# Two interleaved side pipelines of a fused attention and channel-mix kernel, moved from a 12-step to a 14-step beat

## Chip, cores and metric

The kernel runs on one core of one Trainium2 chip. The metric is device time in microseconds (us); less is better. The kernel's main loop has 400 steps of some 2.8 us each.

## What is computed

```python
def mab(q, kv):                          # m = 32 inducing points, C = 128, N = 12608, B = 4
    s = scale * (q @ kv.transpose(0, 2, 1))
    s = s - s.max(-1, keepdims=True)
    a = np.exp(s); a /= a.sum(-1, keepdims=True) + 1e-09
    return a @ kv
h = mab(I, x)                            # 32 pooled rows per batch, needs all of x
x = mab(x, h)                            # every token attends to the 32 rows
x_prev = shift x by one token
xk = mu_k * x + (1 - mu_k) * x_prev;  xr = mu_r * x + (1 - mu_r) * x_prev
k = np.maximum(xk @ w_k, 0)              # 128 -> 1024
out = sigmoid(xr @ w_r) * (k * k @ w_v)  # 1024 -> 128
```

## The kernel before

**The main loop.** The tokens of a batch are cut into 24 groups of 512 and one of 320, and a group's 1024 hidden columns into four units of 256. A step handles one unit of one group, so a batch has 25 x 4 = 100 steps (`UB`) and the program 400, counted n = 0 to 399. In a step TensorE first does the up projection of unit n (four matmuls into `ps_a`, L773 and L775), VectorE takes the positive part into `k_t` (L785), ScalarE squares it twice (`kh`, L790, and the exact square over `k_t`, L791), GpSimd takes the difference `kl` of the two (L793), and TensorE does the down projection of unit n - 4 (six matmuls into `ps_v`, L804). In the steps listed in `high_vector`, VectorE makes `kh` (L787) in place of ScalarE. In steps with n mod 4 = 1 TensorE also computes the gate's input (`zgate`, L762 and L763) into the `ps_v` bank that the group's down projection will use next, and ScalarE reads it for the sigmoid `rT` (L765); the first down matmul of that group, in step n + 3, overwrites the bank and so has to wait for `rT`. VectorE multiplies the finished group by `rT` (`gate`, L809, n mod 4 = 0) and transposes it into the output tile `ot` (L820, n mod 4 = 1). `ot` has one buffer for four groups, stored by four DMAs (L827) in steps 16k + 5; the next four groups begin to fill it in step 16k + 9 and wait for those DMAs.

Every engine executes its instructions in the order in which the Python code issues them. `ps_a` has two buffers, so the up projection of step n + 2 waits for VectorE's reads of step n.

**The side pipelines.** Two chains of small operations are hung into the steps by hand: `at(n, f)` runs f at the end of step n, `soon(n, f)` runs it right after the up projection of step n.

- `stage_a(b, j, at, t)` folds block j (2048 tokens) of batch b into the running softmax of the 32 pooled rows. It transposes the block on VectorE in four pieces (`btr`, L333, into `xs`) and moves each piece by four DMAs into the tiles `xt` (L336); at t + 9 come scores on TensorE (L361, bank `pb_a`) and a maximum on VectorE (L364); `common` (L371, bank `pb_b`) and `running` at t + 11; `expo` on ScalarE at t + 15; a transpose `e1` at t + 17 (L405); `hmm`, 16 small matmuls each, at t + 18 and t + 19 (L426); `acc` at t + 20. The last full block takes the 320 left-over tokens along (`t_scores`, and L370 before `common`), one step later.
- `stage_b(b, j, at, t)` computes the attention of block j's tokens over the finished rows: scores at t (L610, bank `pb_b`, kept until `low`), a softmax over 32 on VectorE with `expo` on ScalarE at t + 3 (L627), a high part `ah` at t + 7 (L650), a low part `al` at t + 9 (L654), and from t + 10 on, four times, `spread(i)`: five DMAs that build the tile `R` of one group (one for its first column out of the group before, L587, and four, L664). The main loop reads `R` in that group's four steps.
- `combine(b)` turns the pooled rows into the batch's weights `W` (t + 9 to t + 15).

All these DMAs and the loads of x go through SyncE's one queue (SP), in order. While the main loop works on batch b, stage A runs on batch b + 1 and stage B on the next blocks of batch b. ScalarE's `Exp` and `Sigmoid` need different tables, so a change from one to the other brings an `ACT_TABLE_LOAD`.

**The beat before** is one block per 12 steps (`SEG = 12`). With t = 100b (t = 4 for batch 0), stage A of block j starts at t + 12j and stage B of block j + 1 at t + 12j + 1; `combine` starts at t + 72 and stage B of the next batch's first block at t + 85.

Of the kernel before, what the change touches and what calls it, by code (L numbers as in the profile page):

```python
# [8 lines left out]
F32 = mybir.dt.float32  # L9
# [10 lines left out]
def kernel(  # L20
# [31 lines left out]
    xt_pool = ctx.enter_context(tc.tile_pool(name="xt_pool", bufs=24))  # L52
    st = ctx.enter_context(tc.tile_pool(name="st", bufs=1))
    wp = ctx.enter_context(tc.tile_pool(name="wp", bufs=2))
    sm = ctx.enter_context(tc.tile_pool(name="sm", bufs=2))
    r_pool = ctx.enter_context(tc.tile_pool(name="r_pool", bufs=10))
    mp = ctx.enter_context(tc.tile_pool(name="mp", bufs=2))
    pa = ctx.enter_context(tc.tile_pool(name="pa", bufs=2, space=bass.MemoryType.PSUM))
    pv = ctx.enter_context(tc.tile_pool(name="pv", bufs=2, space=bass.MemoryType.PSUM))
# [19 lines left out]
    wr_sb = const.tile([P, C], F32, name="wr_sb")  # L79
# [223 lines left out]
    def xt_tile(S, j, i):  # L303

        w = groups(j)[0][1]
        if w == G:
            S.xt[j, i] = xt_pool.tile([P, G], F32, name="xt")
        elif i == 0:
            S.xt_tail = xt_pool.tile([P, TAIL], F32, name="xtl", bufs=1)
            for ii in range(Q):  # L310
                S.xt[j, ii] = S.xt_tail[:, ii * w:(ii + 1) * w]
        return S.xt[j, i]

    def stage_a(b, j, at, t):
# [6 lines left out]
        S = batches[b]  # L321
# [4 lines left out]
        last = 4 if tail else 0  # L326

        def btr(c):
            if c == 0:
                for i in range(Q):  # L330
                    xt_tile(S, j, i)
            xs = st.tile([P, G], F32, name="xs", bufs=3)
            nc.vector.transpose(out=xs.rearrange("p (s q) -> p s q", q=M),  # L333
                                in_=S.xb[j][:, :, M * c:M * (c + 1)])
            for i in range(Q):
                nc.sync.dma_start(out=S.xt[j, i][M * c:M * (c + 1), :], in_=xs[M * i:M * (i + 1)])  # L336

        def t_tr():
            ps = pb_tile("a")
# [65 lines left out]
            nc.vector.transpose(out=L["e1"], in_=L["e1t"].rearrange("p (s q) -> p s q", q=M))  # L405

        def t_etrans():
            ps = pb_tile("b")
            nc.tensor.transpose(out=ps[:tw, :P], in_=L["s1t"], identity=ident)
            L["e1x"] = sm.tile([P, P], F32, name="mk", bufs=1)  # L410
            nc.vector.tensor_copy(out=L["e1x"][:tw], in_=ps[:tw, :P])
# [59 lines left out]
    def combine(b, at=None, t=0):  # L471
# [18 lines left out]
        def weights():  # L490
            ws = S.sum
            if ahead:
                wt = sm.tile([P, 1], F32, name="wt")
                nc.scalar.activation(out=wt, in_=S.mrun, func=AF.Exp, bias=L["nm"], scale=scale)
                ws = sm.tile([P, 1], F32, name="ws")
                nc.vector.tensor_tensor(out=ws, in0=S.sum, in1=wt, op=ALU.mult)
            ps = pb_tile(None if ahead else "b")
            nc.tensor.matmul(out=ps[:, :1], lhsT=stack_f, rhs=ws, start=True, stop=True)
            rd = sm.tile([P, 1], F32, name="rd")
            nc.vector.tensor_scalar(out=rd, in0=ps[:, :1], scalar1=EPS, scalar2=None, op0=ALU.add)  # L500
            nc.vector.reciprocal(out=rd, in_=rd)
            sw = sm.tile([P, P], F32, name="mk", bufs=1)
            if ahead:
                nc.vector.tensor_scalar(out=sw, in0=stack_f, scalar1=wt, scalar2=rd,
                                        op0=ALU.mult, op1=ALU.mult)
            else:
                nc.vector.tensor_scalar(out=sw, in0=stack_f, scalar1=rd, scalar2=None, op0=ALU.mult)
            L["sw"] = sw

        def hfin():  # L510
            ps = pb_tile(None if ahead else "b")
            nc.tensor.matmul(out=ps[:, :P], lhsT=S.acc, rhs=L["sw"], start=True, stop=True)
            h = sm.tile([P, P], F32, name="hT")
# [58 lines left out]

        if ahead:
            return maxes, weights, hfin, wpart
        at(t + 9, weights)
        at(t + 10, hfin)
        parts = [(s, f"k{s}", c * G, wk_sb[:, c * G:(c + 1) * G]) for c in range(F // G) for s in range(2)]
        for n in range(0, len(parts), Q):
            wpack(parts[n:n + Q], G, ("ah", "al", 1), t + 11 + 4 * (n // Q))
        wpack([(s, f"r{s}", F, wr_sb) for s in range(2)], C, ("xs", "xs", 3), t + 13)  # L580

    def halo(S, g, far=True):

# [5 lines left out]
            nc.vector.tensor_copy(out=S.R[g][:, 0:1], in_=S.R[g - 1].bitcast(F32)[:, G:G + 1])  # L589


    def stage_b(b, j, at, t):

# [60 lines left out]
        def spread(i):  # L656
            src = (L["ah"].bitcast(F32), L["al"].bitcast(F32))
            if full or i == 0:
                S.R[j * Q + i] = r_pool.tile([P, G + 1], F32R, name="R")
                halo(S, j * Q + i)  # L660
            R = S.R[j * Q + (i if full else 0)].bitcast(F32)
            o, lo = (0, 0) if full else (offs[i], i * w - offs[i])
            for q in range(Q):
                nc.sync.dma_start(out=R[M * q:M * (q + 1), 1 + o + lo:1 + o + w],  # L664
                                  in_=src[q % 2][M * i:M * (i + 1), lo:w])

        at(t, scores)
        at(t + 1, trans)
        at(t + 1, maxi)
        at(t + 2, sub)  # L670
        at(t + 3, expo)
        at(t + 5, total)
        at(t + 5, recip)
        at(t + 6, mult)
        at(t + 6, back)
        at(t + 7, high)
        at(t + 9, low)
        for i in range(Q):
            at(t + 10 + i, lambda i=i: spread(i))
# [256 lines left out]
    def at(n, f):  # L936
        events.setdefault(n, []).append(f)
# [39 lines left out]
            at(k + 5, put)  # L977
        at(4, lambda: units[0][0].zgate(first=True))

    SEG = 12  # L980
    high_vector = set()
    for b in range(B):
        t = b * UB + (4 if b == 0 else 0)
        for j in range(NBLK - 1):
            s = t + SEG * j
            high_vector |= {s + 4, s + 8}
            if b + 1 < B:
                stage_a(b + 1, j, at, s)
# [78 lines left out]
```

## Time and profile before

| | |
|---|---|
| time, median of 3 runs | 1167.95 us (1167.78 to 1170.74) |
| time of the profiled execution | 1165.47 us |
| its span, first to last instruction | 1163.7 us |
| instructions in the span | 17576 |
| main loop's first step begins at | 54.98 us |
| PE, PEld, DVE, ACT, POOL busy | 96%, 72%, 80%, 83%, 81% |
| mean granted TensorE clock | 0.996 |
| VectorE `kh` steps (L787) | 48 |
| table loads of ScalarE in the sigmoid, stage A and stage B lines (L765, L393 and L394, L627) | 31, 15 and 3, 12 |

PE is TensorE's matmuls and PEld its weight loads, DVE is VectorE, ACT ScalarE, POOL GpSimd, SPq the DMA issues of SyncE's queue. A row of the waits names the waiting engine with its tile and line, then what ended the wait, the total in us, the count and the longest. In the timeline a row has its start, its length and, in brackets, the idle time before it and what ended that. Ends of matmuls are modelled and overlap, so the distance from one start to the next tells more than their lengths.

### The profile page before, as it was taken

To read this page: it belongs to the slowest core of one execution; us is meant where nothing else is said; L and a number is where in the kernel's file an instruction comes from. 1 tells how busy PE (TensorE), PEld (TensorE's weight loads), DVE (VectorE), ACT (ScalarE), POOL (GpSimd) and SP (SyncE) were. 2 spreads that over 40 slices of the span, in tenths; PEclk is the share of its full clock that TensorE was granted. 3 is DMA by queue.
4 is the path that set the end of the run, shared out by engine and by line. 5 is a ranking of instruction groups with operands and counts; after the bars stand their busy time and mean duration, and the time that the engine had idled before them with its cause. 6 is when DMAs were issued, how large, how long until landed. Compare 5 with 4: busy or idle time off the path is not lost.

```text
span 1163.7 us, 17576 instructions
## 1 busy us (share of the span) xinstructions
PE 1114.2 (96%) x5746; PEld 834.2 (72%) x5746; DVE 934.3 (80%) x1259; ACT 970.9 (83%) x1107; POOL 947.7 (81%) x413
## 2 busy tenths in 40 slices
PE   7779999999999999999999999999999999999997
PEld 5456777776677777777767777777768777777886
DVE  5778889887878888888787889897787888887665
ACT  5478888887888888788978988888789888889996
POOL 1158888888787888888879888888878899999997
PEclk9989999999999999999999999999999999999999
DMA  9112554544226455465043554645304314432231
GB/s 288 50 32 75 128 118 106 109 117 92 39 58 134 108 105 123 108 135 120 5 76 74 118 125 104 134 96 124 45 15 82 63 34 73 73 64 46 43 46 34
DMA packets 273515, 102.31 MB, mean 88 GB/s; under 512 B 232816, under 2 KB 248336, under 8 KB 271120
## 3 DMA queue, kind: packets, MB, share of 16 engines
q1 hardware_dynamic: 273088, 101.17, 40.5%
q8 instruction: 46, 0.75, 0.3%
q14 instruction: 45, 0.37, 0.1%
q10 hardware_dynamic: 336, 0.02, 0.0%
HBM read 28.07 MB, written 25.82 MB: 46 GB/s over the span
## 4 chain that ended last, share of the span: by engine, by line
PE 61%; DVE 15%; ACT 8%; SPq 6%; issue 5%; DMA 4%; DVEq 0%; ACTq 0%
PE ps_v L804 31%; PE ps_a L773 11%; PE ps_a L775 10%; DVE k_t L785 5%; SPq L336 2%; DMA out_dram<-ot 2%; ACT kh L790 2%; SPq L827 2%; PE pb_a L426 1%; PE pb_b L610 1%; PE ps_v L762 1%; PE ps_v L763 1%; SPq L664 1%; ACT k_t L791 1%; PE pb_a L361 1%
## 5 line engine op out<-in xcount | busy, mean ns | idle before, releaser
L793 POOL TENSOR_TENSOR kl<-k_t,kh 128x1024 fp32r<-128x1024 f32 (+2 forms) x400 | 939.0, 2375 | 169.0 <-ACT k_t L791 148.9
L785 DVE TENSOR_SCALAR k_t<-ps_a 128x1024 f32<-128x1024 f32 (+1 forms) x400 | 480.9, 1202 | 155.5 <-PE ps_a L775 144.1
L791 ACT ACTIVATE k_t<-k_t 128x1024 f32<-128x1024 f32 (+1 forms) x400 | 418.2, 1048 | 45.5 <-DVE kh L787 34.3
L790 ACT ACTIVATE kh<-k_t 128x1024 fp32r<-128x1024 f32 (+1 forms) x352 | 365.9, 1040 | 104.5 <-DVE k_t L785 57.8
L773 PE MATMUL ps_a<-R,W 128*128 128x512 f32 (+1 forms) x800 | 325.9, 408 | 4.7 <-DMA R<-al 3.4
L775 PE MATMUL ps_a<-R,W 128*128 128x512 f32 (+1 forms) x800 | 313.6, 392 | 0.0
L804 PE MATMUL ps_v<-kh,wvh 128*128 128x512 f32 (+1 forms) x800 | 251.9, 396 | 5.5 <-ACT rT L765 5.0
L804 PE MATMUL ps_v<-kl,wvh 128*128 128x512 f32 (+1 forms) x800 | 249.2, 393 | 0.0
L804 PE MATMUL ps_v<-kh,wvl 128*128 128x512 f32 (+1 forms) x800 | 249.0, 392 | 0.0
L773 PEld LDWEIGHTS ps_a<-R,W 128*128 128x128 f32 x800 | 151.2, 189 | 82.3 <-issue 22.4
L804 PEld LDWEIGHTS ps_v<-kh,wvh 128*128 128x128 f32 x800 | 147.9, 189 | 42.3 <-ACT rT L765 10.1
L804 PEld LDWEIGHTS ps_v<-kl,wvh 128*128 128x128 f32 x800 | 149.6, 188 | 35.5 <-POOL kl L793 0.3
L804 PEld LDWEIGHTS ps_v<-kh,wvl 128*128 128x128 f32 x800 | 149.8, 188 | 34.9
L775 PEld LDWEIGHTS ps_a<-R,W 128*128 128x128 f32 x800 | 151.1, 189 | 29.8
L820 DVE STREAM_TRANSPOSE ot<-oT 128x512 f32<-128x512 f32 x96 | 67.4, 702 | 12.2 <-DMA out_dram<-ot 11.3
L809 DVE TENSOR_TENSOR oT<-ps_v,rT 128x512 f32<-128x512 f32 (+1 forms) x100 | 66.7, 667 | 2.4 <-PE ps_v L804 0.2
L787 DVE SCALAR_TENSOR_TENSOR kh<-ps_a,k_t 128x1024 fp32r<-128x1024 f32 x48 | 58.8, 1225 | 5.4 <-PE ps_v L804 0.5
L765 ACT ACTIVATE rT<-ps_v 128x512 f32<-128x512 f32 (+1 forms) x99 | 57.2, 578 | 0.3
L333 DVE STREAM_TRANSPOSE xs<-xb 128x512 f32<-128x512 f32 x72 | 50.0, 695 | 0.3
L765 ACT ACT_TABLE_LOAD x31 | 39.8, 1283 | 0.6
L762 PE MATMUL ps_v<-R,W 128*128 128x512 f32 (+1 forms) x99 | 38.9, 393 | 0.0
L763 PE MATMUL ps_v<-R,W 128*128 128x512 f32 (+1 forms) x99 | 38.7, 391 | 0.0
(194 smaller groups left out, 643.6 us busy)
## 6 DMA issues: line engine op xcount, KB each, us to landing
out_dram<-ot SPq DMA_DIRECT2D x92, 256.0 KB, 4.4
xb<-in_x_dram SPq DMA_DIRECT2D x18, 1024.0 KB, 5.3
xt<-xs SPq DMA_DIRECT2D x288, 64.0 KB, 2.0
R<-ah SPq DMA_DIRECT2D x184, 64.0 KB, 2.0
R<-al SPq DMA_DIRECT2D x184, 64.0 KB, 2.0
kh<-in_x_dram SPq DMA_DIRECT2D x4, 512.0 KB, 8.2
kl<-in_x_dram SPq DMA_DIRECT2D x4, 512.0 KB, 6.4
xb<-in_x_dram SPq DMA_DIRECT2D x8, 256.0 KB, 5.4
```

The lines of the kernel that those rows point to most:

```text
L762: nc.tensor.matmul(out=ps[:, :w], lhsT=S.W[0][:, F:WF], rhs=R[:, 1:w + 1], start=True, stop=False)
L765: nc.scalar.activation(out=self.rT, in_=ps[:, :w], func=AF.Sigmoid)
L773: nc.tensor.matmul(out=ps[:, c, :w], lhsT=S.W[0][:, cs], rhs=R[:, 1:w + 1], start=True, stop=False)
L775: nc.tensor.matmul(out=ps[:, c, :w], lhsT=S.W[1][:, cs], rhs=R[:, 0:w], start=False, stop=True)
L785: nc.vector.tensor_scalar(out=k, in0=self.ps[:, :, :w], scalar1=0.0, scalar2=None, op0=ALU.max)
L787: nc.vector.scalar_tensor_tensor(out=kh, in0=self.ps[:, :, :w], scalar=0.0, in1=k, op0=ALU.max, op1=ALU.mult)
L790: nc.scalar.activation(out=kh, in_=k, func=AF.Square)
L791: nc.scalar.activation(out=k, in_=k, func=AF.Square)
L793: return lambda eng, a, z: eng.tensor_tensor(out=kl[:, :, a:z], in0=k[:, :, a:z], in1=kh.bitcast(F32)[:, :, a:z], op=ALU.subtract)
L804: nc.tensor.matmul(out=self.v, lhsT=wt[:, fc, :], rhs=kk[:, c, :], start=(fc == 0 and n == 0), stop=(fc == FC - 1 and n == 2))
L809: nc.vector.tensor_tensor(out=self.oT, in0=self.v, in1=self.rT, op=ALU.mult)
L820: nc.vector.transpose(out=ot[:, o:o + w], in_=self.oT)
```

## The change

The work stays the same; the steps in which the side pipelines' operations stand are new, and some table sizes with them.

- **Starts.** For batch 0 the 12-step beat stays, one step earlier (stage A from 3, stage B from 4); stage B's blocks 5 and 6 stand later, at 63 and 77 (before 53 and 65), and the four spreads of block 4 three steps later than its other steps would have it. For batches 1 to 3 the beat is 14: stage A of batch b + 1 at 100b - 9 + 14j, stage B of batch b at 100b + 4 + 14j. Stage A of the batch after next thus begins while `combine` and the first stage B of the next batch still run.
- **Within the stages.** `combine`'s steps are counted from 0 and placed at stage A's last start + 21, the next batch's first stage B at + 25. `btr` is split: the transposes of a block's pieces stand at -2, -1, +1, +3 (batches 2 and 3; before -1, 0, +1, +3), the DMAs of the first two together at -1. The left-over tokens' stage B is drawn together into fewer steps.
- **`kh` on VectorE** in 54 steps (before 48): in batch 0's loop at stage A's start + 4 and + 8, from batch 1 on at + 7 and + 10 and at 80 and 90 of the batch.
- **Buffers.** `R` has 8 tiles instead of 10, the left-over tokens' `xtl` two instead of one. Three short uses of bank `pb_b` go to `pb_a`.

```diff
-    r_pool = ctx.enter_context(tc.tile_pool(name="r_pool", bufs=10))
+    r_pool = ctx.enter_context(tc.tile_pool(name="r_pool", bufs=8))
...
         def btr(c):
+            L["xs", c] = st.tile([P, G], F32, name="xs", bufs=3)
+            nc.vector.transpose(out=L["xs", c].rearrange("p (s q) -> p s q", q=M),
+                                in_=S.xb[j][:, :, M * c:M * (c + 1)])
+
+        def bmove(c):
...
-        for c in range(Q):
-            at(t + (-1, 0, 1, 3)[c], lambda c=c: btr(c))
+        for c, n in enumerate((-2, -1, 1, 3) if b > 1 else (-1, 0, 1, 3)):
+            at(t + n, lambda c=c: btr(c))
+            at(t + max(n, -1), lambda c=c: bmove(c))
...
-    SEG = 12
     high_vector = set()
     for b in range(B):
-        t = b * UB + (4 if b == 0 else 0)
+        t = b * UB
+        if b == 0:
+            first_a = [t + 3 + 12 * j for j in range(NBLK - 1)]
+            first_b = [t + n for n in (4, 16, 28, 40, 63, 77)]
+            high_vector |= {s + n for s in first_a for n in (4, 8)}
+        else:
+            first_a = [t - 9 + 14 * j for j in range(NBLK - 1)]
+            first_b = [t + n for n in (4, 18, 32, 46, 60, 74)]
+            high_vector |= {s + n for s in first_a for n in (7, 10)} | {t + 80, t + 90}
         for j in range(NBLK - 1):
-            s = t + SEG * j
-            high_vector |= {s + 4, s + 8}
             if b + 1 < B:
-                stage_a(b + 1, j, at, s)
-            stage_b(b, j + 1, at, s + 1)
+                stage_a(b + 1, j, at, first_a[j])
+            stage_b(b, j + 1, at, first_b[j], wait=3 if (b, j) == (0, 3) else 0)
         if b + 1 < B:
-            s = t + SEG * (NBLK - 1)
-            combine(b + 1, at, s)
-            stage_b(b + 1, 0, at, s + 13)
+            s = first_a[-1]
+            combine(b + 1, at, s + 21)
+            stage_b(b + 1, 0, at, s + 25)
```

The line numbers move with it: L785 becomes L783, L790 and L791 become L788 and L789, L765 L763, L627 L630, L820 L818, L336 L338, L664 L667, L827 L825.

**SyncE's queue in batch 1, up to its first store.** Before, a group's `R` DMAs and a piece's `xt` DMAs take turns (`xb` is the load of the next block of x, `out_dram` the store):

```order
L587 DMA R<-R 128x1
L664 DMA R<-ah 32x512
L664 DMA R<-al 32x512
L664 DMA R<-ah 32x512
L664 DMA R<-al 32x512
L336 DMA xt<-xs 32x512 x4
L205 DMA xb<-in_x_dram 128x2048
L827 DMA out_dram<-ot 32x64x32 x4
```

Now, at the same store:

```order
L590 DMA R<-R 128x1
L667 DMA R<-ah 32x512
L667 DMA R<-al 32x512
L667 DMA R<-ah 32x512
L667 DMA R<-al 32x512
L338 DMA xt<-xs 32x512 x12
L825 DMA out_dram<-ot 32x64x32 x4
L338 DMA xt<-xs 32x512 x4
L205 DMA xb<-in_x_dram 128x2048
```

The four spreads of a block follow each other, and the block's `xt` DMAs come after all of them.

**VectorE around step 157**, where the first group of a new `ot` is transposed and stage A's scores of a block are reduced (`mx`). Before, steps 156 and 157:

```order
L785 TENSOR_SCALAR k_t<-ps_a 128x1024
L787 SCALAR_TENSOR_TENSOR kh<-ps_a,k_t 128x1024
L441 SCALAR_TENSOR_TENSOR acc<-acc,alpha,pb_a 128x128
L785 TENSOR_SCALAR k_t<-ps_a 128x1024
L820 STREAM_TRANSPOSE ot<-oT 128x512
L364 TENSOR_REDUCE mx_5328<-pb_a 128x1
```

Now, steps 156 and 157:

```order
L783 TENSOR_SCALAR k_t<-ps_a 128x1024
L366 TENSOR_REDUCE mx_5267<-pb_a 128x1
L783 TENSOR_SCALAR k_t<-ps_a 128x1024
L785 SCALAR_TENSOR_TENSOR kh<-ps_a,k_t 128x1024
L818 STREAM_TRANSPOSE ot<-oT 128x512
```

The reduction now stands a step ahead of the transpose that can wait for a store.

**ScalarE where both stages take their exponentials** (`e1t` is stage A's, `s` stage B's, `rT` the sigmoid). Before, steps 127 to 129:

```order
L791 ACTIVATE k_t<-k_t 128x1024
L393 ACT_TABLE_LOAD
L393 ACTIVATE alpha<-mkr,nb 128x1
L394 ACTIVATE e1t,ss<-pb_a,nb 128x512
L791 ACTIVATE k_t<-k_t 128x1024
L627 ACTIVATE s_4414<-s_4414 128x512
L790 ACTIVATE kh<-k_t 128x1024
L791 ACTIVATE k_t<-k_t 128x1024
L765 ACT_TABLE_LOAD
L765 ACTIVATE rT<-ps_v 128x512
```

Now, steps 120 and 121:

```order
L789 ACTIVATE k_t<-k_t 128x1024
L395 ACT_TABLE_LOAD
L395 ACTIVATE alpha<-mkr,nb 128x1
L396 ACTIVATE e1t,ss<-pb_a,nb 128x512
L788 ACTIVATE kh<-k_t 128x1024
L789 ACTIVATE k_t<-k_t 128x1024
L763 ACT_TABLE_LOAD
L763 ACTIVATE rT<-ps_v 128x512
L630 ACT_TABLE_LOAD
L630 ACTIVATE s_4217<-s_4217 128x512
```

The sigmoid of step 121 now stands between the two exponentials, with a table load on each side, and the next sigmoid, in step 125, has a third. The same happens around steps 149, 221 and 249; in the other blocks of batches 1 and 2 both exponentials stand between two sigmoids.

More of the change, by code (lines that the diff above doesn't have):

```diff
@@ L308, in xt_tile @@
         elif i == 0:
-            S.xt_tail = xt_pool.tile([P, TAIL], F32, name="xtl", bufs=1)
+            S.xt_tail = xt_pool.tile([P, TAIL], F32, name="xtl", bufs=2)
             for ii in range(Q):
@@ L331, in btr @@
                     xt_tile(S, j, i)
-            xs = st.tile([P, G], F32, name="xs", bufs=3)
-            nc.vector.transpose(out=xs.rearrange("p (s q) -> p s q", q=M),
-                                in_=S.xb[j][:, :, M * c:M * (c + 1)])
             for i in range(Q):
-                nc.sync.dma_start(out=S.xt[j, i][M * c:M * (c + 1), :], in_=xs[M * i:M * (i + 1)])
+                nc.sync.dma_start(out=S.xt[j, i][M * c:M * (c + 1), :], in_=L["xs", c][M * i:M * (i + 1)])
         def t_tr():
@@ L407, in t_etrans @@
         def t_etrans():
-            ps = pb_tile("b")
+            ps = pb_tile("a")
             nc.tensor.transpose(out=ps[:tw, :P], in_=L["s1t"], identity=ident)
@@ L443, in acc @@
             S.xb.pop(j)
-        for c in range(Q):
-            at(t + (-1, 0, 1, 3)[c], lambda c=c: btr(c))
+        for c, n in enumerate((-2, -1, 1, 3) if b > 1 else (-1, 0, 1, 3)):
+            at(t + n, lambda c=c: btr(c))
+            at(t + max(n, -1), lambda c=c: bmove(c))
         if tail:
-            at(t + 5, t_tr)
+            at(t + (7 if b > 1 else 5), t_tr)
             soon(t + 11, t_scores)
@@ L496, in weights @@
                 nc.vector.tensor_tensor(out=ws, in0=S.sum, in1=wt, op=ALU.mult)
-            ps = pb_tile(None if ahead else "b")
+            ps = pb_tile(None if ahead else "a")
             nc.tensor.matmul(out=ps[:, :1], lhsT=stack_f, rhs=ws, start=True, stop=True)
@@ L510, in hfin @@
         def hfin():
-            ps = pb_tile(None if ahead else "b")
+            ps = pb_tile(None if ahead else "a")
             nc.tensor.matmul(out=ps[:, :P], lhsT=S.acc, rhs=L["sw"], start=True, stop=True)
@@ L574, in combine @@
             return maxes, weights, hfin, wpart
-        at(t + 9, weights)
-        at(t + 10, hfin)
+        at(t, weights)
+        at(t + 1, hfin)
         parts = [(s, f"k{s}", c * G, wk_sb[:, c * G:(c + 1) * G]) for c in range(F // G) for s in range(2)]
         for n in range(0, len(parts), Q):
-            wpack(parts[n:n + Q], G, ("ah", "al", 1), t + 11 + 4 * (n // Q))
-        wpack([(s, f"r{s}", F, wr_sb) for s in range(2)], C, ("xs", "xs", 3), t + 13)
+            wpack(parts[n:n + Q], G, ("ah", "al", 1), t + 2 + 4 * (n // Q))
+        wpack([(s, f"r{s}", F, wr_sb) for s in range(2)], C, ("xs", "xs", 3), t + 4)
     def halo(S, g, far=True):
@@ L589, in halo, with stage_b @@
             nc.vector.tensor_copy(out=S.R[g][:, 0:1], in_=S.R[g - 1].bitcast(F32)[:, G:G + 1])
-    def stage_b(b, j, at, t):
+    def stage_b(b, j, at, t, wait=0):
         S = batches[b]
@@ L665, in spread @@
                                   in_=src[q % 2][M * i:M * (i + 1), lo:w])
[L667 to L679, printed above, removed]
+        moves = [lambda i=i: spread(i) for i in range(Q)]
+        steps = ((0, scores), (1, trans), (1, maxi), (2, sub), (3, expo), (5, total), (5, recip), (6, mult),
+                 (6, back), (7, high), (9, low), *((10 + wait + i, f) for i, f in enumerate(moves)))
+        if not full:
+            steps = ((0, scores), (1, trans), (1, maxi), (1, sub), (2, expo), (3, total), (3, recip), (3, mult),
+                     (3, back), (4, high), (5, low), *((6 + i // 2, f) for i, f in enumerate(moves)))
+        for n, f in steps:
+            at(t + n, f)
     def stage_b_head(gs):
```

## The prediction

> **What bounds the kernel now.** I read the page's busy times first, then the windows over one 12-step block in the middle of batch 1.
>
> ```profile
> PE 1114.2 (96%) x5746; PEld 834.2 (72%) x5746; DVE 934.3 (80%) x1259; ACT 970.9 (83%) x1107; POOL 947.7 (81%) x413
> 414.50:448.10 33.60, 33.60 (x177) 24.67 (x176) 29.81 (x41) 28.76 (x32) 28.74 (x14) 1.00 0.39 102
> ```
>
> In the block from 414.50 to 448.10 TensorE is busy for all 33.60 us; VectorE, ScalarE and GpSimd have 4 to 5 us to spare. The change takes nothing from TensorE, so it can win only TensorE's waits outside such blocks. The view of the waits names them:
>
> ```profile
> PE pb_a L736 <- DVE W L537: 6.5, 1, 6.5
> PE ps_v L804 <- ACT rT L765: 5.0, 7, 1.2
> PE pb_b L371 <- DVE mx L370: 4.0, 3, 1.8
> PE ps_a L773 <- DMA R<-al: 3.4, 2, 2.1
> PE pb_b L371 <- DVE al L654: 1.9, 2, 1.2
> PE pb_a L426 <- DVE e L405: 1.4, 2, 1.2
> ...
> PEld ps_v L804 <- ACT rT L765: 10.1, 11, 1.6
> PEld pb_b L371 <- DVE al L654: 3.3, 3, 1.6
> PEld pb_a L426 <- DVE e L405: 2.8, 3, 1.7
> PEld pb_a L361 <- DMA xt<-xs: 1.7, 3, 1.0
> ```
>
> PE counts a wait from the modelled end of the last matmul and is a low count, the weight loads begin to wait earlier and are a high one; where both stand I take about their middle. 6.5 belongs to the start-up. The rest, some 20 us or 1.8%, is what a new placing can reach.
>
> Two mechanisms stand behind it. The first is SyncE's queue. Timeline of SP, then of VectorE and TensorE, around step 57 of batch 0:
>
> ```profile
> 215.73 2.44 SPq L336 DMA_DIRECT2D xt<-xs  x4
> 218.27 5.55 SPq L827 DMA_DIRECT2D out_dram<-ot  x4
> 223.87 1.45 SPq L587 DMA_DIRECT2D R<-R  x1
> ...
> 227.24 0.71 DVE L820 STREAM_TRANSPOSE ot<-oT 128x512 f32<-128x512 f32 x1 [1.89 <-DMA out_dram<-ot]
> 227.88 0.67 DVE L405 STREAM_TRANSPOSE e<-e1t 128x512 f32<-128x512 f32 x1
> ...
> 228.60 0.65 PE L426 MATMUL pb_a<-xb,e 128*32 128x128 f32 x16 [1.23 <-DVE e L405]
> ```
>
> The queue issues a DMA every 0.6 us (2.44 for four). Stage A's and stage B's DMAs meet in the same steps, the store is issued late behind them, VectorE waits 1.89 us for it with `e` behind, and TensorE waits 1.23 us for `e`. VectorE has six such waits:
>
> ```profile
> DVE ot L820 <- DMA out_dram<-ot: 11.3, 6, 2.7
> ```
>
> The waits for `al`, `e` and `xt` above and one of those for `mx` follow from this queue. The second mechanism is ScalarE's table reloads, here in steps 104 to 108 (batch 1):
>
> ```profile
> 361.76 1.28 ACT L627 ACT_TABLE_LOAD   x1
> 363.05 0.63 ACT L627 ACTIVATE s<-s 128x512 f32<-128x512 f32 x1
> 363.59 1.04 ACT L790 ACTIVATE kh<-k_t 128x1024 fp32r<-128x1024 f32 x1
> ...
> 365.75 1.28 ACT L765 ACT_TABLE_LOAD   x1
> 367.04 0.60 ACT L765 ACTIVATE rT<-ps_v 128x512 f32<-128x512 f32 x1
> ...
> 364.03 0.63 PE L804 MATMUL ps_v<-kh,wvh 128*128 128x512 f32 x2
> ...
> 365.44 0.39 PE L773 MATMUL ps_a<-R,W 128*128 128x512 f32 x1
> ...
> 367.69 0.74 PE L804 MATMUL ps_v<-kh,wvh 128*128 128x512 f32 x2 [1.16 <-ACT rT L765]
> ```
>
> A load and exponential hold ScalarE 1.83 us (361.76 to 363.59), the two squares of a step 2.16 (363.59 to 365.75), load and sigmoid 1.88. With two loads in two adjacent steps `rT` is 1.16 us late for the down projection three steps after it. TensorE's six down matmuls from 364.03 to 365.44 are 0.235 apart, so a step of ten takes 2.35.
>
> **The change part by part.** *R tiles, 3.4.* Both waits come where a spread stands one step before its need, steps 16 and 100. Now the first `R` of blocks (0,1) and (1,0) is spread in steps 14 and 98, a step earlier. Low part to use took 3.3 us in step 14 to 16 (SP, then PE):
>
> ```profile
> 104.31 0.51 SPq L664 DMA_DIRECT2D R<-al  x1
> 107.63 0.46 PE L773 MATMUL ps_a<-R,W 128*128 128x512 f32 x1 [1.31 <-DMA R<-al]
> ```
>
> A step (2.35 us; less in the narrow group before step 100) covers 1.31 whole and the 2.1 nearly. I leave 0.5 at step 100: gain 2.9.
>
> *Queue waits.* In batches 1 and 2 spreads now stand at 0 to 3 and `xt` moves at 4, 4, 6, 8 of the 14 steps; in batch 0 the store of step 53 is issued before the delayed spreads, and the one of step 21 follows the crowd by one step more. There are as many DMAs as before. Without `xt` moves between them, spreads have to wait for each other's landing (the first column comes from the group before), as in batch 3 now:
>
> ```profile
> 934.25 0.51 SPq L587 DMA_DIRECT2D R<-R  x1
> ...
> 938.83 0.51 SPq L587 DMA_DIRECT2D R<-R  x1
> ```
>
> 4.6 us per spread, so four take 18 us, from step 13's low part to about step 19 of a block; the eight moves of step 18 (5 us) then end near step 21, the store of step 21 near 24 and its landing before step 25 fills `ot` again. It fits, narrowly. The next stores stand further from the spreads. Also, `e` and `mx` of the block now stand ahead of the waiting transpose on VectorE. I take all of it as gone: `xt` 1.7, `e` 2.1 (1.4 to 2.8), `al` 2.6 (1.9 to 3.3): gain 6.4. If that cover fails, it stays.
>
> *The left-over tokens' maximum (`mx` L370), 4.0.* On VectorE `gate` and L370 stand in the chain to `common`, and TensorE has nothing to do meanwhile:
>
> ```profile
> 277.23 0.69 DVE L809 TENSOR_TENSOR oT<-ps_v,rT 128x512 f32<-128x512 f32 x1
> 277.84 1.93 DVE L370 TENSOR_TENSOR mx<-mx,mx 128x1 f32<-128x1 f32 x1
> ```
>
> One step later (one earlier in batch 0) `gate` falls outside: three times 0.69, gain 2.0 of 4.0, with 0 to 4.0 as the ends.
>
> *`rT` waits, 7.5 (5.0 to 10.1).* Where these stand now (steps 12, 96, 108, 192, 208, 292, 308 and on in batch 3), the exponential comes two or more steps ahead of the sigmoid's load, or the sigmoid comes first. Each step in between gives ScalarE back at least 2.35 - 2.16; at 108 the next `kh` step and the later stage B help. I take 7.5 as gone, then add what is new.
>
> *New: four double reloads* (steps 120 to 125, 148 to 153, and the same in batch 2). Stage A's exponential on ScalarE, and VectorE's `k_t`:
>
> ```profile
> 425.71 1.28 ACT L393 ACT_TABLE_LOAD   x1
> ...
> 427.87 1.05 ACT L791 ACTIVATE k_t<-k_t 128x1024 f32<-128x1024 f32 x1
> ...
> L785 DVE TENSOR_SCALAR k_t<-ps_a 128x1024 f32<-128x1024 f32 (+1 forms) x400 | 480.9, 1202 | 155.5 <-PE ps_a L775 144.1
> ```
>
> ScalarE's work from `kh` of step 120 to `rT` of step 125: six steps of 2.16, 13.0; stage A's exponential with load, alpha and sum, 2.16 (425.71 to 427.87); sigmoid with load 1.88; stage B's exponential with load 1.83; sigmoid with load 1.88: 20.7. TensorE from the end of step 120's up projection to that of step 128's: eight steps of 2.35, 18.8; two gates of two matmuls, 0.9; two `hmm` of 0.65, 1.3: 21.0. ScalarE can start one matmul and one `k_t` (1.2) after that first end, at 1.4, or at 2.2 if VectorE is late by some 0.8 (my estimate: one 0.67 operation of stage A or B more), as side work in steps 119 and 120 makes likely. So step 128's down projection waits 1.1 (20.7 + 1.4 - 21.0) to 1.9; I take 1.6, nearer to the late start: four times, cost 6.4.
>
> [...] The trace has the load's 1.28 and the exponential 0.01 after it, no drain. [...]
>
> *New: the batch boundaries.* Stage A of the batch after next now transposes four pieces beside stage B and the weights, in steps 89 to 94 and 189 to 194, with `kh` on VectorE in 190:
>
> ```profile
> 70.74 0.71 DVE L333 STREAM_TRANSPOSE xs<-xb 128x512 f32<-128x512 f32 x1
> ```
>
> Four times 0.71 makes VectorE's `k_t`, and so `rT` of step 93 and 193, later by up to 2; `ps_a`'s second buffer hides part. I take 0.7 each, 0 to 2: cost 1.4. *Start:* the first of these transposes now stands in step 2, in the chain for which TensorE waits the 6.5: cost 0.7.
>
> *At nothing:* six more `kh` on VectorE and the smaller ring of `R`. VectorE has 3.8 us to spare in the block above, and by the step numbers an `R` tile is written again nine steps after its group's last one or later; if that failed, its spread would hold the queue.
>
> **The sum.** 2.9 + 6.4 + 2.0 + 7.5 - 6.4 - 1.4 - 0.7 = 10.3 us. The profiled execution took 1165.47 (span 1163.7 and 1.8 around it), which gives 1155.2. The median of the runs stands 2.5 higher, at 1167.95; the new median should be 1167.95 - 10.3 = 1157.6.
>
> **The rivals.** *The queue stays late.* The uncovered spreads hold the queue 18 us per block, so the stores still come late: 6.4 stays, and half of the R gain. 1165.5. For it: as many DMAs, 4.6 us per spread; against it: the moves no longer share their steps.
>
> *The reloads cost nothing,* because `kh` steps and the slower steps around give ScalarE time, and the boundaries are hidden too: 1157.6 - 6.4 - 1.4 = 1149.8.
>
> *Slower: the double reload does not recover.* With ScalarE 8 us behind, GpSimd falls behind it, and the down projections of steps 124 to 128 wait for `kl` too; the next block's reload begins before the queue is empty. It decides the sign from (10.3 + 6.4) / 4 = 4.2 us per place; at 5.5 the time is 1173. Against it: the six steps before the next pair of exponentials give back 0.2 to 0.8 each, and the second of two reloading blocks is 28 steps away.
>
> *A reload that costs double.* If each of the four loads at such a place held ScalarE another 1.28, the wait would grow by 5.1 at four places, to 1178. [...]
>
> *It doesn't do what it says:* the order of instructions moved, but waits that I count as gone only change their names, within 0.3% (3.5 us, about what a measurement can tell from no change): 1166.
>
> **How the numbers follow.** Forecast (1153 to 1162) 0.60; no cost of reloads 0.14; queue stays late 0.12; slower by reloads 0.06; double load 0.01; renamed waits 0.07. Faster by over 0.3%: 0.60 + 0.14, and half of the late queue, whose span reaches below 1164.4: 0.80. Same: the other half and the renamed waits, 0.13. Slower: 0.07. The range 1149 to 1166 holds the forecast, nearly all of the low rival, the late queue and half of the renamed waits, about 0.85.
>
> **What would show it.** Right: the waits for `R`, `xt`, `e`, `al` gone or below 1 us in sum, and VectorE's waits for the store too; L371 behind `mx` near 2 us; TensorE waiting for `rT` four times, in steps 128, 156, 228 and 256, some 1.6 us each; four more table loads than before; batch 3 without waits for `rT`. Wrong: a wait for the store that remains in batches 1 and 2, waits of TensorE for `kl`, or a long wait in steps 90 to 100.

## The result and the profile after

The changed kernel is slower: 1201.12 us median of 4 runs (1200.80 to 1202.86) beside 1168.28 for the kernel before on the same chip (4 runs, 1167.78 to 1170.74). The ratio is 1.0280, with a 95% interval of 1.0262 to 1.0298. The forecast was 1157.6, with a range up to 1166, so it missed the sign, and by 43.5 us. The profiled execution has a span of 1199.5 us against 1163.7. One execution of experiment 7's kernel took 1548.0 us at a granted clock of 0.655, where all other runs have 0.98 or more, and its median below is that of the other three.

The page after, the busy times:

```profile
PE 1126.2 (94%) x5746; PEld 837.0 (70%) x5746; DVE 933.6 (78%) x1265; ACT 972.2 (81%) x1105; POOL 946.6 (79%) x413
```

No engine has more work: VectorE, ScalarE and GpSimd are within 1.5 us of before. TensorE shows 12 us more for the same 5746 matmuls (some ran slower, see the end; the mean granted clock is 0.984, before 0.996), and the rest of the 36 us is waiting. The view of the waits after, the rows that answer to those of the prediction and the largest new ones:

```profile
PE ps_a L771 <- DVE k_t L783: 18.0, 7, 7.7
...
PE ps_v L760 <- DVE oT L807: 5.0, 6, 3.1
...
PE pb_b L373 <- DVE mx L372: 4.6, 3, 2.0
...
PE pb_a L343 <- ACT e1t L396: 2.1, 1, 2.1
PE pb_a L363 <- DMA xt<-xs: 2.1, 2, 1.2
...
PE pb_b L373 <- DVE al L657: 1.5, 1, 1.5
...
PE ps_v L802 <- ACT rT L763: 1.0, 5, 0.3
...
PE ps_a L771 <- DMA R<-al: 0.7, 1, 0.7
...
DVE ot L818 <- DMA out_dram<-ot: 2.9, 3, 1.7
```

Much of what was forecast to go has gone: TensorE's wait for `R` is 0.7 (3.4 before), for `rT` 1.0 (5.0), and VectorE's wait for the store 2.9 (11.3). In their place TensorE waits 18.0 us for `k_t` and 5.0 for `oT`, both of which VectorE makes. The groups of VectorE, the transposes of stage A, before (L333) and after (L330): count, busy and mean time, then the idle time ahead of them and what ended it.

```profile
L333 DVE STREAM_TRANSPOSE xs<-xb 128x512 f32<-128x512 f32 x72 | 50.0, 695 | 0.3
```

```profile
L330 DVE STREAM_TRANSPOSE xs<-xb 128x512 f32<-128x512 f32 x72 | 50.1, 696 | 39.0 <-DMA W<-xs 16.3 <-DMA xb<-in_x_dram 11.2 <-DMA xt<-xs 10.8
```

VectorE works in order, and these transposes now hold it for 39.0 us where they held it for 0.3. The first of the two longest is at the first batch boundary, step 92 (timeline after: SyncE's queue, then VectorE, then TensorE):

```profile
319.60 6.22 SPq L825 DMA_DIRECT2D out_dram<-ot  x4
325.92 3.08 SPq L568 DMA_DIRECT2D W<-ah  x2
...
340.44 2.49 SPq L568 DMA_DIRECT2D W<-xs  x4
...
342.94 0.71 DVE L330 STREAM_TRANSPOSE xs<-xb 128x512 f32<-128x512 f32 x1 [8.05 <-DMA W<-xs]
343.58 1.19 DVE L783 TENSOR_SCALAR k_t<-ps_a 128x1024 f32<-128x1024 f32 x1
...
344.82 0.80 PE L771 MATMUL ps_a<-R,W 128*128 128x512 f32 x1 [7.67 <-DVE k_t L783]
```

From 319.60 to 342.9 the queue issues a store and 24 DMAs of packed weights almost without a pause. Eight of these (`W<-xs`) read two of the three `xs` tiles; `combine` packs the receptance part there. Stage A of the batch after next wants a third tile and then these two, waits 8.05 us, `k_t` stands behind it, and TensorE stops for 7.67. The second boundary shows the same (8.20 on VectorE in step 192, 6.68 on TensorE in step 193). In steps 64 and 205 the transposes wait for a load of `xb` that was issued late, in 166 and 266 for late `xt` moves:

```profile
225.63 2.72 SPq L590 DMA_DIRECT2D R<-R  x1
...
242.84 0.51 SPq L590 DMA_DIRECT2D R<-R  x1
...
245.94 0.58 SPq L205 DMA_DIRECT2D xb<-in_x_dram  x1
...
251.16 0.71 DVE L330 STREAM_TRANSPOSE xs<-xb 128x512 f32<-128x512 f32 x1 [4.60 <-DMA xb<-in_x_dram]
```

Each `R<-R` is the first column of a spread; the first and the last of a block's four are shown. It waits for the landing of the group before, and all that stands behind it in the queue waits with it; the load of `xb` comes 20 us after the first of them. The queue's waits ahead of a spread, before (L587) and after (L590), sum, times and longest:

```profile
SPq L587 <- DMA R<-al: 19.4, 25, 1.6
...
SPq L587 <- DMA R<-ah: 11.1, 14, 0.9
SPq L587 <- PE ps_v L804: 6.4, 12, 1.7
...
SPq L587 <- PE ps_a L775: 4.7, 5, 2.5
```

```profile
SPq L590 <- DMA R<-al: 65.6, 68, 4.8
...
SPq L590 <- DMA R<-ah: 35.2, 36, 4.1
...
SPq L590 <- PE ps_a L773: 4.6, 5, 1.8
...
SPq L590 <- PE ps_v L802: 2.4, 6, 0.6
...
SPq L590 <- PE ps_v L761: 1.4, 1, 1.4
```

The waits for landings have grown from 30.5 in sum (19.4 and 11.1) to 100.8. Those for TensorE's last use of an `R` tile have not, 8.4 in sum after 11.1.

### The profile page after: what moved, and what is told of

Read it like the earlier page. It is cut to its first block, busy times and chain, and to the rows that moved or that the text cites. A ratio compares the mean times of both kernels' runs of the same rounds, so it can differ in the third digit from the quotient of the medians.

```text
span 1199.5 us, 17594 instructions
## 1 busy us (share of the span) xinstructions
PE 1126.2 (94%) x5746; PEld 837.0 (70%) x5746; DVE 933.6 (78%) x1265; ACT 972.2 (81%) x1105; POOL 946.6 (79%) x413
## 4 chain that ended last, share of the span: by engine, by line
PE 68%; DVE 10%; ACT 8%; issue 5%; SPq 5%; DMA 4%; POOL 0%; DVEq 0%; ACTq 0%; POOLq 0%
PE ps_v L802 34%; PE ps_a L771 13%; PE ps_a L773 12%; DVE k_t L783 4%; ACT kh L788 3%; PE pb_b L613 2%; PE pb_a L363 2%; PE ps_v L760 2%; PE ps_v L761 2%; ACT k_t L789 1%; PE pb_a L428 1%; DMA xt<-xs 1%; SPq L667 1%; DMA R<-al 1%; DMA xb<-in_x_dram 1%
## 5 line engine op out<-in xcount | busy, mean ns | idle before, releaser
L791 POOL TENSOR_TENSOR kl<-k_t,kh 128x1024 fp32r<-128x1024 f32 (+2 forms) x400 | 937.9, 2375 | 205.6 <-ACT k_t L789 161.6
L783 DVE TENSOR_SCALAR k_t<-ps_a 128x1024 f32<-128x1024 f32 (+1 forms) x400 | 479.2, 1199 | 125.3 <-PE ps_a L773 118.7
L788 ACT ACTIVATE kh<-k_t 128x1024 fp32r<-128x1024 f32 (+1 forms) x346 | 360.6, 1042 | 133.6 <-DVE k_t L783 79.3
L789 ACT ACTIVATE k_t<-k_t 128x1024 f32<-128x1024 f32 (+1 forms) x400 | 419.2, 1048 | 49.4 <-DVE kh L785 38.1
L330 DVE STREAM_TRANSPOSE xs<-xb 128x512 f32<-128x512 f32 x72 | 50.1, 696 | 39.0 <-DMA W<-xs 16.3
L818 DVE STREAM_TRANSPOSE ot<-oT 128x512 f32<-128x512 f32 x96 | 67.1, 699 | 7.0 <-issue 3.9
L785 DVE SCALAR_TENSOR_TENSOR kh<-ps_a,k_t 128x1024 fp32r<-128x1024 f32 (+1 forms) x54 | 64.9, 1203 | 6.0 <-PE ps_v L802 0.5
L763 ACT ACTIVATE rT<-ps_v 128x512 f32<-128x512 f32 (+1 forms) x99 | 57.3, 579 | 0.4
L760 PE MATMUL ps_v<-R,W 128*128 128x512 f32 (+1 forms) x99 | 40.8, 412 | 5.0 <-DVE oT L807 5.0
L761 PE MATMUL ps_v<-R,W 128*128 128x512 f32 (+1 forms) x99 | 39.7, 401 | 0.0
```

The costliest lines, as they stand in the source:

```text
L760: nc.tensor.matmul(out=ps[:, :w], lhsT=S.W[0][:, F:WF], rhs=R[:, 1:w + 1], start=True, stop=False)
L763: nc.scalar.activation(out=self.rT, in_=ps[:, :w], func=AF.Sigmoid)
L783: nc.vector.tensor_scalar(out=k, in0=self.ps[:, :, :w], scalar1=0.0, scalar2=None, op0=ALU.max)
L785: nc.vector.scalar_tensor_tensor(out=kh, in0=self.ps[:, :, :w], scalar=0.0, in1=k, op0=ALU.max, op1=ALU.mult)
L788: nc.scalar.activation(out=kh, in_=k, func=AF.Square)
L789: nc.scalar.activation(out=k, in_=k, func=AF.Square)
```

## The experiments

The first theory, T1: SyncE's queue is late, because of the spreads that wait and of the W DMAs, and VectorE's transposes carry that to `k_t`. Its rival, T2: the boundary has too much work for VectorE, whatever waits.

**Experiment 1: the receptance pack in tiles of its own.**

```
-        wpack([...], C, ("xs", "xs", 3), t + 4)
+        wpack([...], C, ("wh", "wl", 1), t + 4)
```

> The kernel after, but the small rest of the packed weights (two columns) gets two small tiles of its own and no longer takes two of the three xs tiles. Theory T1 (VectorE, which works in order, is held in its transposes xs<-xb by W DMAs that stand late in SyncE's queue; k_t behind it is late and TensorE stops): the 8 us waits at steps 92 and 192 vanish, 1201 - (16 +/- 3) = 1185 us. Rival T2 (the batch boundary has too much VectorE work of stage A, stage B and the weights, whatever waits): 1198 to 1201.

(The tiles hold 128 columns, by a `max(cw, C)` in place of `G` inside `wpack`, not the two that this text names.) Measured: 1195.94 us, ratio 1.0226 (1.0200 to 1.0252), 5 us less, which is between the two expectations. The 16.3 for `W<-xs` is gone; other waits of the same transposes grew:

```profile
L330 DVE STREAM_TRANSPOSE xs<-xb 128x512 f32<-128x512 f32 x72 | 50.1, 696 | 28.3 <-DMA xt<-xs 15.4 <-DMA xb<-in_x_dram 12.4 <-DMA xl<-in_x_dram 0.2
```

The named wait was real and worth a third of what T1 gave it: the queue stayed late, and the transposes wait for the next DMA in it.

**Experiment 2: the first column moved last in each spread.**

```
-                halo(S, j * Q + i)
...
+            if full or i == 0:
+                halo(S, j * Q + i)
```

> The kernel after, but each spread issues its first-column DMA behind its four R moves instead of ahead of them, so that no spread holds SyncE's queue until the moves of the group before have landed. T1: spreads 3.0 us apart instead of 4.6; the loads of xb and the xt moves behind them come earlier, VectorE's waits at steps 64, 166, 205 and 266 shrink, those at 92 and 192 in part: 1186 to 1193 us. T2: same as the kernel after, 1201 within 2.

Measured: 1190.44, ratio 1.0189 (1.0164 to 1.0213), as T1 expected. VectorE's waits at the transposes are 25.2 us (`W<-xs` still 16.9).

**Experiment 3: both edits.**

> Both edits together: own tiles for the rest of the packed weights, and the first column moved last. T1: nearly all of the loss goes, 1166 to 1176 us, with the shift at step 200 against the kernel of before under 10 us. T2: 1196 to 1201. If the two edits cure the same waits, the sum is smaller than their parts: about 1185.

Measured: 1180.70, ratio 1.0110 (1.0079 to 1.0142). The waits at the transposes fell to 14.8 and T2 has fallen, but the time is above the range of T1 too: 12 us more is left than in the kernel before.

**Experiment 4: without the new `kh` on VectorE in steps 80 and 90.**

```
-            high_vector |= {s + n for s in first_a for n in (7, 10)} | {t + 80, t + 90}
+            high_vector |= {s + n for s in first_a for n in (7, 10)}
```

> The kernel after without its new kh on VectorE in the steps 80 and 90 of a batch (six fewer vector squares; ScalarE makes them). T1: 1201 within 1.5, since the waits come from DMAs. T2 (VectorE has too much to do at the boundary): 5 us or more less, 1196 or below.

Measured: 1206.41, ratio 1.0322 (1.0297 to 1.0346). That is 5 us above what T1 expected, and further still from T2: without these six operations on VectorE the kernel is not faster, so they are not the cause. How much of the 5 us more belongs to the edit stays open: its profile is 3 us behind that of the changed kernel already at step 90, where the two programs are still the same.

**Experiments 5 and 6: the two halves of the change.** Batch 0 placed as before and the rest as after, and the other way round (`first_a`, `first_b` and the places of `combine` of one half set back; the code and the pools as after).

> The kernel after, but batch 0 keeps the places that its blocks have in the kernel of before (every 12 steps from step 4, spreads not delayed); batches 1 and 2 as in the kernel after. T1 (several places of batch 0 and each boundary cost by themselves): the loss of steps 40 to 90, some 9 us, goes and the boundaries stay: 1189 to 1194 us. If the late spreads and the store of batch 0 also make the wait at step 92, that goes too: 1182 to 1187. T2 (the loss is all in batches 1 and 2): 1199 to 1202.

> The kernel after, but batches 1 and 2 keep the 12 steps of the kernel before; batch 0 as in the kernel after. T1: what batch 0's new places cost alone, 1168 + 9 = 1177 us, within 3. T2: 1168 within 2.

Measured: 1197.76 (1.0232 to 1.0273) and 1196.06 (1.0218 to 1.0261). Both halves keep most of the loss, experiment 5 lies outside both expectations, and both theories fail in experiment 6, whose batches 1 and 2 stand where they stood before. There `ot` waits for its store again, in the waits of VectorE:

```profile
DVE ot L818 <- DMA out_dram<-ot: 27.1, 12, 6.5
```

In the kernel before it was 11.3. This sent me to batch 3, where no stage A stands and the work of the two kernels is nearly the same. A store there, before and after:

```profile
1042.15 4.26 SPq L827 DMA_DIRECT2D out_dram<-ot  x4
```

```profile
1035.65 5.93 SPq L825 DMA_DIRECT2D out_dram<-ot  x4
```

The same four DMAs of the same size hold the queue 39% longer, and the other batches have longer stores too. For all 108 DMAs from `ot`, shortest, median and longest time in the queue in ns, before and after:

```profile
L827 SPq DMA_DIRECT2D out_dram<-ot x108: 315/984/2036, 128.5 to 1158.9; - x108
```

```profile
L825 SPq DMA_DIRECT2D out_dram<-ot x108: 315/1514/4497, 127.2 to 1194.8; - x108
```

What differs is where `ot` lies. A tile of the `R` ring takes 2080 bytes per partition; two tiles fewer and one `xtl` of 1280 more move everything in the pool of `ot` by 2880 bytes, which is 22.5 times 128. In the built programs `ot` is at 165376, a multiple of 128, before and at 162496, 64 bytes off one, after. The store reads `ot` in pieces of 32 floats, 128 bytes. That is theory T3.

**Experiments 7 and 8: batch 0 as before on top of experiment 3, and a control.** Experiment 8 is the kernel before with the first column moved last.

> The kernel of experiment 3 (own tiles for the rest of the packed weights, first column moved last) with batch 0 placed as before. T1: both edits and the old places of batch 0 add up: 1181 - 7 = 1174 us, within 3. If batch 0's places were cured by the two edits already: 1180.

> A control: the kernel before with the first column moved last in each spread. There the xt moves between the spreads cover the landing, so T1 expects no change: 1168 within 2.5 us. If holding SyncE's queue costs the old placing too, 1165 or below, and experiment 2's gain is then no evidence about the change.

Measured: 1180.81 (ratio 1.0105, 1.0083 to 1.0128) and 1168.46 (1.0001, 0.9990 to 1.0013). So batch 0's places cost nothing that shows once the two edits are in, and moving the column last gains nothing in the kernel before: the held queue is a cost of the new placing.

**Experiments 9 and 10: only the address of `ot`.** One line, in the kernel after and in the kernel before:

```
     mp = ctx.enter_context(tc.tile_pool(name="mp", bufs=2))
+    mp.tile([P, 16], F32, name="gap", bufs=1)
```

> The kernel after with an unused tile of 64 bytes per partition ahead of ot, so that ot lies at a multiple of 128 bytes as in the kernel of before (address 162560 instead of 162496); nothing else is changed. Theory T3 (smaller R ring and other tile sizes moved ot off a 128-byte boundary; each store then holds SyncE's queue 6.2 us instead of 4.4, and all that stands behind it is late): the four DMAs of a store take 4.4 us again, and with T1's waits shortened the time falls by 10 to 20, to 1181 to 1191 us. Rival T4 (the stores are slower for their place in the program, or the ring of 8 and the PSUM banks cost): the stores stay at 6.2, 1199 to 1202.

> The kernel before with the same unused tile of 64 bytes ahead of ot, which moves ot off the 128-byte boundary (165440 instead of 165376); nothing else is changed. T3: the four DMAs of a store take 6.2 us instead of 4.4; by what experiment 6 lost in batches 1 to 3, where its blocks stand as before, some 10 to 20 us: 1178 to 1188. T4: 1168 within 2.5.

Measured: the kernel after falls to 1187.91, ratio 1.0161 (1.0138 to 1.0185); the kernel before rises to 1185.35, ratio 1.0142 (1.0122 to 1.0161). T3 holds both ways, inside what it expected, and T4 falls. The stores of the kernel after with the gap, and of the kernel before with it:

```profile
L826 SPq DMA_DIRECT2D out_dram<-ot x108: 315/1000/4630, 127.2 to 1182.2; - x108
```

```profile
L828 SPq DMA_DIRECT2D out_dram<-ot x108: 315/1462/2947, 131.0 to 1178.2; - x108
```

The gap moves `kh`, `k_t`, `kl`, `oT` and `rT` off the boundary as well. The operations on them take as long as before (VectorE's `k_t` 1202 ns in the kernel before with and without the gap; GpSimd's `kl` 2375 and ScalarE's exact square 1048 in the kernels before and after, and in the latter these tiles are off the boundary too), and the `xt` and `R` moves still land after 2.0 us, so it is the store that costs.

In the kernel before with the gap the late queue shows where the first part of the prediction found it, and more than doubled: VectorE's wait for the store was 11.3 in six places, TensorE's for `e` 1.4 and for `al` 1.9.

```profile
DVE ot L821 <- DMA out_dram<-ot: 24.5, 11, 4.7
...
PE pb_b L372 <- DVE al L655: 5.7, 3, 2.2
PE pb_a L427 <- DVE e L406: 5.2, 3, 1.8
```

**Experiments 13 and 14: which shift.** Gaps of 128 and of 32 bytes in the kernel before.

> The kernel before with an unused tile of 128 bytes ahead of ot, so that everything in mp is moved and ot is still at a multiple of 128. If the boundary decides (T3): stores of 4.4 us, 1168 within 2.5 us. If any shift of the tiles does it: 1178 to 1186.

> The kernel before with an unused tile of 32 bytes ahead of ot, so that each 128-byte piece of a store crosses a boundary after 96 bytes instead of 64. If crossing decides: stores of 6.2 us, 1182 to 1189. If only a multiple of 64 that is not one of 128 is slow: 1168 within 2.5.

Measured: 1169.33 (ratio 1.0003, 0.9987 to 1.0019) and 1191.50 (1.0181, 1.0151 to 1.0211), the second above its range. The issue rows give KB and median us to landing, for 128 and then 32 bytes:

```profile
out_dram<-ot SPq DMA_DIRECT2D x92, 256.0 KB, 4.4
```

```profile
out_dram<-ot SPq DMA_DIRECT2D x92, 256.0 KB, 5.2
```

So it is the boundary and not the moving: both offsets that make the 128-byte pieces cross it cost. The median DMA of a store takes 1456 ns at 32 bytes and 1462 at 64, so the stores do not tell why the kernel lost 21 us at 32 bytes and 17 at 64; that stays open.

**Experiments 11, 15 and 12: what is left.** Experiment 15 is the kernel after with the gap and the column moved last; 11 has the tiles for the receptance pack as well; 12 is 11 with two steps placed anew.

```
-            at(t + (7 if b > 1 else 5), t_tr)
+            (at if b > 1 else soon)(t + (7 if b > 1 else 6), t_tr)
...
-            s = first_a[-1]
+            s = first_a[-1] - (b > 0)
```

> The kernel after with ot back on the boundary and the first column moved last, the rest of the packed weights still in the xs tiles. Experiment 2 gained 10.7 us with slow stores; if that is mostly the held queue: 1188 - 10 = 1178 us, within 3, and the W DMAs are worth the other 6. If the faster stores had cured the same waits: 1183 to 1187.

> Experiment 3 (own tiles for the rest of the packed weights, first column moved last) with ot back on a 128-byte boundary. T1 and T3 together: 1181 - 12 = 1169 us, within 5, so about the kernel before; if the forecast's gains of the new placing are left over, 1158 to 1164. T4: 1180 to 1182.

> Experiment 11 with two steps placed anew: the transpose of the left-over tokens in batch 0 one step later and ahead of hmm (it waits 2.3 us in step 68 for ScalarE's exponential to leave its PSUM bank), and the weights and the first stage B of the next batch one step earlier in batches 1 and 2 (TensorE waits 2.4 us in step 200 for an R tile). If these waits are what keeps experiment 11 above the kernel before: 1172.3 - 2.3 - 2.4 = 1167.6 us, within 2. If they only hide other waits: 1171 to 1173.

Measured: 1182.21 (ratio 1.0111, 1.0086 to 1.0135), 1172.31 (1.0041, 1.0027 to 1.0056) and 1167.99 (0.9985, 0.9972 to 0.9997). The first lies between its two expectations: the column gained 6 of the 10. The other two came as expected. Experiment 12 is the first form of the changed kernel that is not slower than the kernel before; it is faster by 0.15%, which the interval barely tells from nothing. What it mended in step 68, as the timeline of experiment 11 shows it:

```profile
253.46 0.62 PE L804 MATMUL ps_v<-kl,wvh 128*128 128x512 f32 x2
256.18 0.50 PE L344 MATMUL pb_a<-ident,xl 80*128 80x80 f32 x4 [2.10 <-ACT e1t L397]
```

The transpose of the left-over tokens writes the PSUM bank `pb_a`, in the kernel before as here, and `pb_a` holds the scores of the block before until ScalarE's exponential has read them. In both kernels the transpose stands two steps behind that exponential; in the kernel before, in steps 67 and 69, it did not wait. Here, in steps 66 and 68, the exponential ends 2 us too late. In the profile after VectorE is held for `xb` in step 64 (the 4.60 us above) and ScalarE waits 4.97 us behind it; whether this makes the exponential late was not tried. VectorE's idle time ahead of the transposes, in experiment 15, 11 and 12:

```profile
L331 DVE STREAM_TRANSPOSE xs<-xb 128x512 f32<-128x512 f32 x72 | 50.0, 695 | 19.5 <-DMA W<-xs 15.5 <-DMA xb<-in_x_dram 3.5 <-DMA xt<-xs 0.4
```

```profile
L331 DVE STREAM_TRANSPOSE xs<-xb 128x512 f32<-128x512 f32 x72 | 50.0, 694 | 9.7 <-DMA xb<-in_x_dram 5.1 <-DMA xt<-xs 4.5
```

```profile
L331 DVE STREAM_TRANSPOSE xs<-xb 128x512 f32<-128x512 f32 x72 | 50.0, 695 | 8.8 <-DMA xb<-in_x_dram 6.0 <-DMA xt<-xs 2.7
```

The start of the first up matmul of a step, against the kernel before's profile (us; "end" is the last matmul's end):

| step | before | after | exp. 10 | exp. 9 | exp. 15 | exp. 11 | exp. 12 |
|---|---|---|---|---|---|---|---|
| 0 | 55.0 | +0.5 | +2.6 | +0.8 | +0.7 | -0.4 | +0.4 |
| 40 | 175.2 | +0.5 | +4.0 | -0.3 | -0.9 | -2.8 | -1.7 |
| 90 | 320.3 | +9.7 | +9.2 | +6.2 | +3.7 | +0.5 | +1.6 |
| 100 | 346.3 | +17.3 | +9.2 | +12.0 | +10.5 | +0.9 | +2.0 |
| 190 | 601.6 | +20.8 | +13.8 | +14.2 | +9.1 | +1.8 | +2.8 |
| 200 | 624.8 | +29.4 | +13.9 | +21.8 | +17.5 | +4.9 | +3.1 |
| 300 | 902.8 | +37.8 | +19.1 | +25.0 | +18.3 | +7.2 | +3.4 |
| end | 1157.5 | +35.9 | +19.3 | +23.3 | +16.7 | +5.6 | +2.2 |

(The head before step 0 differs by up to 3 us from one execution to the next, and the kernel before's profile is 2.8 us below its median.) Read down a column: in experiment 9 and 15 the boundaries, steps 90 to 100 and 190 to 200, still cost 6 to 8 us each, and with the pack out of the `xs` tiles they cost 0.4 and 3.1 (experiment 11), then 0.4 and 0.3 (experiment 12). By the ratios, times the 1169 us of the kernel before, the loss of 33 us came off in this order: `ot` back on the boundary 14, the column last 6, the pack's tiles 8, the two steps 6.5. In another order the shares differ: with slow stores the column alone was worth 10.6 and the pack's tiles alone 6.3, or 9.2 on top of the column. These are mostly waits behind one queue, and here its cures did not simply add.

## Why the prediction was wrong

- **"At nothing: ... the smaller ring of `R`"** is the step that failed most: the smaller ring was put at nothing, and by moving `ot` it cost 14 us. The ring itself was large enough, as the prediction said: a spread waits no longer than before for a free `R` (8.4 us in all, before 11.1). But a smaller pool moves what lies behind it, and `ot` came off the 128-byte boundary. Each full store then held SyncE's queue longer, 5.93 us against 4.26 in batch 3. This alone is 14 us in the kernel after and 17 in the kernel before (experiments 9 and 10, with 13 and 14 as the tests of the boundary). "There are as many DMAs as before" was true; that they take as long as before was assumed.
- **"It fits, narrowly"** is the second. The size was about right, 4.6 us from one uncovered spread to the next (more behind a block's first), and the store did fit, even the longer one: the three waits for it that are left stand in steps 26, 90 and 374, none in batch 1 or 2. But the reckoning followed only the `xt` moves and the store. It left out the load of `xb` in the same queue and VectorE's transposes, which wait for that load and for the `xt` moves. Experiments 2, 8 and 15: the held queue costs 6 to 11 us, none of it in the kernel before.
- **"The batch boundaries ... cost 1.4"** took the four transposes at 0.71 each, as work, and asked nothing of the tiles they write. Two of the three `xs` tiles are still being read by W DMAs at the end of a long queue. The wait was 8 us where 0.7, at most 2, was reckoned, at both boundaries, and with it the named sign of a wrong forecast, "a long wait in steps 90 to 100", came true.
- **Not costed at all:** the PSUM bank `pb_a`. The left-over tokens' transpose waits 2.1 us for it in step 68. The three short uses that the change moves to this bank bring a wait of their own: `hmm` of the last block waits, in steps 179 and 279, until VectorE has copied `mk` out of it, 1.8 us in all.
- **Queue waits, 6.4:** the store's wait on VectorE fell from 11.3 to 2.9 and TensorE's for `e` is gone; for `al` 0.4 of 1.9 came, for `xt` nothing. In experiment 9, with fast stores, the wait for the store is 0.4. The waits moved rather than went: from `ot` to `xs`, where the in-order engine holds `k_t` as well.
- **R tiles, 2.9:** came (3.4 to 0.7; that of step 16 is gone). In experiments 3 and 11 the sum is 4.0 again, in steps 100 and 200, where TensorE arrives sooner than in the kernel after; in experiment 12 1.8 is left, in step 100.
- **`mx`, 2.0 of 4.0:** did not come in the kernel after, 4.6: batch 0's wait fell from 1.8 to 0.7, those of batches 1 and 2 rose from 1.1 to 2.0. It is 3.2 in experiment 12, where the latter are 1.3.
- **`rT`, 7.5, less 6.4 for the new double reloads:** both too large. By the middle of the two counts the waits for `rT` fell from 7.5 to 3.4 (1.0 for the matmuls and 5.7 for the weight loads), so 4 came, not 7.5. Four more table loads came, as forecast, but no wait for `rT` of 0.25 us or more stands in steps 128, 156, 228 and 256. What the reloads leave is a wait for `oT` of 0.4 at the gate matmuls of steps 125, 153, 225 and 253, 1.6 in all where 6.4 was reckoned. Experiment 12 has the same four. So neither of the slower rivals, a double reload that does not recover and a load that costs double, occurred. No run shows the other 1.28 us that the second of them laid on a load: in the profile after, the 65 loads at the sigmoid and in the two stages took 1.283 each, and the next operation began 0.01 to 0.02 later.
- **The start, 0.7:** step 0 begins 0.5 us later, less than profiles differ there; it can't be told.
- **The sum:** with the five edits of experiment 12, 1.8 us of the forecast 10.3 are there. The five waits that were counted on (`rT`, `mx`, `R`, `al` and `e`, TensorE's low counts) fell from 15.7 to 6.8 in sum. Others came in their place, 7.6 with two small ones, mostly at the gates and at the bank `pb_a`, which `combine` and `hmm` now share:

```profile
PE pb_a L502 <- DVE acc L444: 2.7, 2, 1.4
PE ps_v L762 <- DVE oT L809: 2.3, 6, 0.5
...
PE pb_a L429 <- DVE mk L414: 1.5, 2, 0.7
```

So even with the side effects mended the new placing comes out where the rival "It doesn't do what it says" put it: most of the waits changed their names.

The forecast's chance of 0.07 for slower came from ScalarE's reloads alone. The mechanism that decided most stood in the list of edits that cost nothing.

## What to carry to other kernels

When an edit changes a pool's size or the number of its buffers, look up where the tiles behind it come to lie. Here `ot`, which the store reads in pieces of 128 bytes, came to lie 64 bytes off a multiple of 128, and the store shown from batch 3 then took 39% longer (5.93 us against 4.26), though nothing in the program says so. Compare the time of one and the same DMA in a part of the program that the edit leaves alone; here that comparison showed the effect directly. And before a step is moved ahead on an in-order engine, follow each buffer that it writes to the last reader of its old contents, down the queue in which that reader stands.

## What was not expected of the hardware

A store of four DMAs in 128-byte pieces took 4.05 to 5.55 us of SyncE's queue (median 4.4) in the kernel before, with its tile at a multiple of 128 bytes, and 5.64 to 8.68 us (median 6.1) in the kernel after, with it 64 bytes off (22 stores each, all but the last ones); 32 bytes off in the kernel before, the median DMA took as long as at 64 (1456 and 1462 ns, 984 on the boundary), and a shift by 128 bytes cost nothing (988).

TensorE came back slow from the waits at the two batch boundaries. Windows after, around step 93: the column behind the five engines is the granted clock.

```profile
332.00:345.00 13.00, 5.33 (x24) 3.98 (x23) 4.95 (x7) 2.66 (x4) 4.96 (x3) 0.90 0.31 74
345.00:352.00 7.00, 7.00 (x22) 5.54 (x23) 6.03 (x9) 6.88 (x8) 3.25 (x2) 0.70 0.42 99
```

```profile
345.42 0.63 PE L773 MATMUL ps_a<-R,W 128*128 128x512 f32 x1
345.84 0.63 PE L771 MATMUL ps_a<-R,W 128*128 128x512 f32 x1
...
349.74 0.40 PE L771 MATMUL ps_a<-R,W 128*128 128x512 f32 x1
349.97 0.40 PE L773 MATMUL ps_a<-R,W 128*128 128x512 f32 x1
```

After 7.7 us without work the matmuls start 0.43 us apart, and from 349.74 on 0.23, so about ten of them lose 0.2 each: by an estimate from these distances, this wait cost some 2 us more than itself. The granted clock from 345 to 350 us is 0.57. After the wait of 6.7 us at the second boundary matmuls are 0.43 apart again, for some 2.5 us, and the clock from 636 to 640 us is 0.57 as well.
